# Attention and two MLPs on one core: the first batch of attention in program order on TensorE, with idle matmuls, the remaining weight decoding queued behind it, and half of the later normalizations on ScalarE

## The chip, the cores and the metric

One Trainium2 chip, one core. The time is device microseconds of one execution; the kernel before has a median of 905.58 us over 3 runs (903.2 to 906.58). The trace is that of one further, profiled execution.

## What is computed

Three stages, each on the output of the one before (2176 tokens, 512 features):

```
# attention: 4 batches x 8 heads, 512 local + 32 global positions, head size 64
s_l = [q_l k_g^T, q_l k_l^T within a window of 32]; out_l = softmax(s_l / 8) [v_g, v_l]
out_g = softmax(q_g [k_g, k_l]^T / 8) [v_g, v_l]
# first MLP: 512 -> 2048 -> 512; the weights arrive as float64
h = x @ w_in;  g = max(h, 0) + alpha * min(h, 0);  x = g @ w_out
# second MLP: 8 experts of 272 tokens each, tokens assigned greedily by x @ w_gate
out[mask_e] = max(x[mask_e] @ w1[e], 0) @ w2[e]
```

The softmax divides by the sum plus 1e-9: each row of exponentials is multiplied by a reciprocal. That multiplication is the "normalization" below.

## The kernel before

**Attention** works on 16 units, each two heads of one batch; four units make a batch (UPB = 4). A unit has two halves j of 256 queries. `attention()` (L473) is a generator that runs through steps n: scores of half n (`scores`, L356: four products, a fused scale, mask and row minimum on VectorE at L376, exponentials with row sums on ScalarE at L378), normalization of half n-1 (`norm`, L381: sum plus 1e-9, reciprocal, and four multiplications of 128x224 on VectorE at L389), transposes of half n-1 on TensorE with copies to SBUF on ScalarE (`ptrans`, L391), products with the values of half n-2 (`pv`, L402) and a copy to the batch's output tile XB. For every pair of units the global queries have a chain of their own, spread over four later steps by `todo` and `one()`: `gscores` (L412), `gnorm` (L429), `gtrans` (L435), `gpv` (L449). It goes to VectorE five times; `gpv` ends in a VectorE copy to XB (L461).

**The first MLP** runs on chunks of 272 tokens, two per batch (`gemm`, L175): a split of the input into a high half (ScalarE) and a low half (VectorE) at `splitx`, then eight slices f of a first product (`gemm1`, L158, 12 matmuls each, L167), each followed by two VectorE instructions (L172, L186) and a split (ScalarE and GpSimd), then a second product (L200), which needs all slices. It goes through half of the 2048 inner features at a time.

**Decoding**: the weights are float64 in memory. `decode` (L73) loads 128x512 of them as pairs of int32 (three raw buffers), takes the magnitude on ScalarE (L78), and puts a float32 together in four VectorE instructions (L79, L81, L82, L83; two magnitude buffers); `split` (L66) rounds on ScalarE and subtracts on GpSimd. `win_part` and `wout_part` are such decodings. The first half of the features needs 8 + 8 of them.

**Order**: batch 0 of the attention runs alone (`alone[0]`, with PSUM pools pS and pX of its own, and bank "y" of pY for the rest); in that loop (L531) four decodings are traced, one in six yields. Then a loop (L549) advances attention and MLP in turns and traces one of the twelve remaining decodings with each turn of the MLP. What is traced earlier has the higher priority, but the framework's planner orders each engine's queue by a timeline of its own: an instruction whose inputs are ready may be put ahead of ones traced before it, on TensorE as on VectorE. Each queue is then worked off in order. Loads and stores are issued by SyncE, also in order.

Of the kernel before, what the change touches and what calls it, by code (L numbers as in the profile page):

```python
# [11 lines left out]
BF = mybir.dt.bfloat16  # L12
# [3 lines left out]
OP = mybir.AluOpType  # L16
# [9 lines left out]
def tile_attention_moe_moe(ctx: ExitStack, tc: tile.TileContext, qkw, vw,  # L26
                           w_in, w_out, alpha, w_gate, w1, w2, out):
    nc = tc.nc
    V, A, P, T = nc.vector, nc.scalar, nc.gpsimd, nc.tensor
    B, H, S, D, SG = BHSDG  # L30
    DM, DF = w_in.shape
    E, _, FF = w1.shape
# [4 lines left out]
    KD = DM // 128  # L37
# [266 lines left out]
    with ExitStack() as at:  # L304
        mk = at.enter_context(tc.tile_pool(name="mk", bufs=1, side="right"))
# [4 lines left out]
        dc = at.enter_context(tc.tile_pool(name="dc", bufs=1, side="right"))  # L310
# [3 lines left out]
        alone = [True]  # L314
# [3 lines left out]
        def bank(shape, name):  # L318
            pool, tag = pY, "y"
            if not alone[0]:  # L320
                pool, tag = pA[0], "a"
            elif name == "s":
                pool, tag = ((pS, "s"), (pS, "s"), (pH, "h1"), (pH, "h1"))[turn[0] % 4]
                turn[0] += 1
            elif name == "t":
                pool, tag = pX, "x"
            return pool.tile(shape, F32, name=name, tag=tag)
# [3 lines left out]
        U = [dict() for _ in units]  # L331
# [14 lines left out]
        def load_v(u):  # L346
            d = U[u]
            vv = ld.tile([128, 2, NB, 2 * D], F32, name="vv", bufs=4)
            nc.sync.dma_start(out=vv.rearrange("p a i d -> p (a i d)"), in_=vw[u])
            d["va"], d["vb"] = vv[:, 0], vv[:96, 1]  # L350
# [30 lines left out]
        def norm(u, j):  # L381
            d = U[u]
            sm = d["sm"][:, :, 2 * j:2 * j + 2]
            V.tensor_scalar(sm, sm, 1e-9, None, op0=OP.add)
            V.reciprocal(sm, sm)
            for ii in range(2):
                i = 2 * j + ii
                for h in range(2):
                    V.tensor_scalar(d["pr"][:, h, i], d["pr"][:, h, i], d["sm"][:, h, i:i + 1], None, op0=OP.mult)  # L389

        def ptrans(u, j, half):  # L391
            d = U[u]
            n = 96 if half else 128
            t = bank([n, 2, 2, 128], "t")
            for ii in range(2):
                for h in range(2):
                    p = d["pr"][:, h, 2 * j + ii]
                    T.transpose(t[:, ii, h], p[:, 128:KW] if half else p[:, 0:128], ident)
            d["t", j, half] = tp.tile([n, 2, 2, 128], F32, name="pt", tag="bt" if half else "at")
            A.copy(d["t", j, half], t)  # L400

        def pv(u, j):  # L402
            d = U[u]
            o = bank([128, 2, 128], "o")
            for ii in range(2):
                i = 2 * j + ii
                for half, v in enumerate(("va", "vb")):
                    for h, c in heads(u):
                        T.matmul(o[c, ii], d[v][:, i, c], d["t", j, half][:, ii, h], start=half == 0, stop=half == 1)
            A.copy(d["x"][:, SG + 256 * j:SG + 256 * j + 256], o.rearrange("p i t -> p (i t)"))  # L410
# [58 lines left out]
            done[0] = 2 * p + 1  # L469

        done = [-1]

        def attention():  # L473
            todo = []

            def one():
                if todo:
                    x, f = todo.pop(0)
                    f()
                    yield x  # L480

            for n in range(2 * NU + 2):
                u, j = divmod(n, 2)
                if u < NU:
                    if j == 0 and u + 2 < NU:
                        load(u + 2)
                        load_v(u + 2)
                    scores(u, j)
                    yield 1.0
                if 1 <= n <= 2 * NU:  # L490
                    a_ = divmod(n - 1, 2)
                    norm(*a_)
                    ptrans(*a_, 0)
                    yield 0.45
                    ptrans(*a_, 1)
                    yield 0.45
                yield from one()
                if n >= 2:
                    pv(*divmod(n - 2, 2))
                    yield 1.0  # L500
                    v, j2 = divmod(n - 2, 2)
                    if v % 2 and j2:
                        gout(v // 2)
                        yield 0.1
                if u < NU and u % 2 == 0 and j:
                    p = u // 2
                    todo += [(0.8, lambda p=p: (gscores(p, 0), gscores(p, 1))), (0.0, lambda p=p: gnorm(p)),
                             (0.6, lambda p=p: (gtrans(p, 0), gtrans(p, 1))), (1.2, lambda p=p: gpv(p))]
# [2 lines left out]
        load(1)  # L511
        load_v(0)
        load_v(1)
        mask = mk.tile([128, 3, KW], F32, name="mask")
        P.memset(mask, 0.0)
        for i in range(3):
# [10 lines left out]
        UPB = H // 2  # L527
        parts = [(win_part, i) for i in range(2 * KD)]
        att = attention()
        n = 0  # L530
        while done[0] < UPB - 1:  # L531
            next(att)
            n += 1
            if n >= 6 and n % 6 == 0 and len(parts) > KD:
                f, i = parts.pop(0)
                f(dc, 0, i)
        nc.sync.dma_start(out=al, in_=alpha.rearrange("(f p) -> p f", p=128))
        nc.sync.dma_start(out=wg, in_=w_gate.rearrange("(k p) e -> p k e", p=128))
        parts += [(wout_part, i) for i in range(KH)]
        alone[0] = False  # L540
        first.close()
        pA.append(at.enter_context(tc.tile_pool(name="pA", bufs=4, space=PSUM)))
        loadx(0, 0)
# [5 lines left out]
        while going:  # L549
            want = c if g is None else c + 1  # L550
            if want < NCH and (want, 0) not in X and done[0] >= (want // CPB + 1) * UPB - 1 and (
                    g is None or len(X[c, 0]) == 4):
                loadx(want, 0)
            if g is None and (c, 0) in X:
                g = gemm(c, 0, None)
            if spent["a"] <= spent["g"] * ratio or g is None:
                x = next(att, None)
                if x is None:
                    going = False
                else:  # L560
                    spent["a"] += x
            else:
                x = next(g, None)
                if x is None:
                    g = None
                    c += 1
                else:
                    spent["g"] += x
                    if parts:
                        f, i = parts.pop(0)  # L570
                        f(dc, 0, i)

    wb = ctx.enter_context(tc.tile_pool(name="wb", bufs=1, side="right"))
    half_tiles(wb, "wb", 1)
# [1 line left out]
    with tc.tile_pool(name="dc2", bufs=1, side="right") as dc, tc.tile_pool(name="pW", bufs=2, space=PSUM) as pW:  # L576
        more = []
        parts = [(win_part, i) for i in range(2 * KD)] + [(wout_part, i) for i in range(KH)]
        n = 0
        while c < NCH:  # L580
# [4 lines left out]
            while next(g, None) is not None:  # L585
                n += 1
                if n % 3 == 0 and parts:
                    f, i = parts.pop(0)
# [12 lines left out]
    with ExitStack() as mo:  # L601
# [84 lines left out]
        for i, n in enumerate(TH + [1]):  # L686
            t = spot(n).bitcast(I32) if i else rc_.tile([128, n], I32, name="jt0")
# [488 lines left out]
        for k in range(E):  # L1176
            n = 0.0
# [86 lines left out]
```

## Time and profile before

| | |
|---|---|
| median of 3 runs | 905.58 us (903.2 to 906.58) |
| profiled execution | 907.86 us, of which the trace spans 906.1 us |
| busy: TensorE, VectorE, ScalarE, GpSimd | 852.9, 544.2, 404.5, 423.4 us |
| mean granted TensorE clock | 0.973 of full speed (2.4 GHz; the lower level is 0.50, 1.2 GHz) |
| DMA | 107.66 MB, mean 119 GB/s |

In the rows, PE is TensorE's matmul part, DVE is VectorE, ACT ScalarE, POOL GpSimd, SP SyncE. A row of the timeline gives the start and the duration in us, engine, line, operation, output <- input, shapes and count; in brackets stands how long the engine had been idle before and which engine's work ended the wait. A row that groups instructions gives the busy time in us and the mean of one in ns. L68 and L67 are the two lines of `split`.

### The profile page before, as it was taken

The page shows a single profiled execution, that of the slowest core. Times are in us where ns is not written, and L with a number is a line of the kernel's source. Part 1 is how long each engine was busy: PE and PEld are TensorE (multiplying, and loading weights), DVE is VectorE, ACT ScalarE, POOL GpSimd, SP SyncE. Part 2 cuts the span into 40 slices and gives each one's busy share as a digit, 9 for nine tenths or more (in the row PEclk, how much of TensorE's full clock was granted, in tenths as well). Part 3 has the DMA queues.
Part 4 walks back from the last instruction along what each step waited for, and adds up shares of the span by engine and source line. Part 5 has one row for each costly group of instructions (what it writes and reads, how often), then busy time and mean ns, then how long its engine had stood idle before and what let it go on. Part 6 is the DMA issues. An engine that isn't in the chain of part 4 may idle for free.

```text
span 906.1 us, 18734 instructions
## 1 busy us (share of the span) xinstructions
PE 852.9 (94%) x7168; PEld 779.2 (86%) x7168; DVE 544.2 (60%) x1783; ACT 404.5 (45%) x945; POOL 423.4 (47%) x367
## 2 busy tenths in 40 slices
PE   5979999999998899999999999999799999899996
PEld 3667888888887899999999899998498898899995
DVE  5999755565629984345555756677476666621120
ACT  5966654554534442233333334331244444444531
POOL 1234211110206543356666865652568678768721
PEclk8968999999999899999999999999999999999999
DMA  8575224223035522023220215332445555455510
GB/s 290 170 250 199 87 78 152 85 74 124 32 102 157 164 88 68 25 64 99 61 88 1 75 49 176 109 119 71 130 146 168 160 168 182 143 179 170 170 41 36
DMA packets 50273, 107.66 MB, mean 119 GB/s; under 512 B 6728, under 2 KB 23112, under 8 KB 50184
## 3 DMA queue, kind: packets, MB, share of 16 engines
q1 hardware_dynamic: 47288, 97.56, 34.4%
q0 software_dynamic: 2896, 8.92, 2.7%
q8 instruction: 56, 0.92, 0.4%
q14 instruction: 33, 0.27, 0.1%
HBM read 88.63 MB, written 17.83 MB: 117 GB/s over the span
## 4 chain that ended last, share of the span: by engine, by line
PE 30%; DMA 9%; POOL 8%; issue 5%; ACT 3%; DVE 2%; POOLq 0%; ACTq 0%
PE h L1106 11%; PE h L167 10%; DMA raw<-in_moe_w_dram 9%; POOL m L68 6%; PE lp L239 3%; ACT m L67 2%; PE h L980 2%; PE h L996 2%; POOL xg L931 1%; PE yt L228 1%; PE y L200 1%; PE pc L820 1%; DMA x2d<-yr 0%; POOL out_dram L1030 0%; PE pa L832 0%
## 5 line engine op out<-in xcount | busy, mean ns | idle before, releaser
L68 POOL TENSOR_TENSOR m<-raw,m 128x1024 fp32r<-128x1024 f32 x64 | 152.8, 2392 | 51.2 <-ACT m L67 50.7
L167 PE MATMUL h<-xh,win 128*128 128x272 f32 x768 | 168.6, 299 | 4.6 <-DVE g L186 2.7
L68 POOL TENSOR_TENSOR glo<-g,ghi 128x272 fp32r<-128x272 f32 x64 | 57.3, 898 | 193.1 <-ACT ghi L67 189.8
L167 PEld LDWEIGHTS h<-xh,win 128*128 128x128 f32 x768 | 128.8, 192 | 12.5 <-DVE g L186 4.4
L167 PE MATMUL h<-xl,win 128*128 128x272 f32 x384 | 112.7, 294 | 1.9 <-DVE xl L68 1.9
L200 PE MATMUL y<-ghi,wout 128*128 128x272 f32 x512 | 112.3, 299 | 2.1 <-ACT ghi L67 2.0
L172 DVE TENSOR_SCALAR nm<-h,al 128x272 f32<-128x272 f32 x128 | 63.4, 497 | 82.6 <-PE h L167 82.0
L1106 PE MATMUL h<-gr,wout 128*128 128x272 f32 x768 | 110.7, 295 | 0.4 <-POOL gr L68 0.4
L980 PE MATMUL h<-xsh,m 128*128 128x272 f32 x512 | 106.9, 298 | 2.0 <-ACT xsh L67 2.0
L67 ACT CAST m<-raw 128x1024 fp32r<-128x1024 f32 x64 | 66.9, 1048 | 85.8 <-DMA raw<-in_moe_w_dram 85.7
L996 PE MATMUL h<-hh,m 128*128 128x272 f32 x512 | 103.3, 293 | 0.0
L1106 PEld LDWEIGHTS h<-gr,wout 128*128 128x128 f32 x768 | 99.3, 188 | 1.3 <-POOL gr L68 0.7
L200 PEld LDWEIGHTS y<-ghi,wout 128*128 128x128 f32 x512 | 84.6, 190 | 6.1 <-ACT ghi L67 2.7
L980 PEld LDWEIGHTS h<-xsh,m 128*128 128x128 f32 x512 | 83.4, 191 | 3.0 <-ACT xsh L67 2.8
L996 PEld LDWEIGHTS h<-hh,m 128*128 128x128 f32 x512 | 81.4, 188 | 0.6 <-issue 0.4
L200 PE MATMUL y<-glo,wout 128*128 128x272 f32 x256 | 76.1, 300 | 2.8 <-POOL glo L68 2.8
L167 PEld LDWEIGHTS h<-xl,win 128*128 128x128 f32 x384 | 73.9, 192 | 2.9 <-DVE xl L68 2.6
L996 PE MATMUL h<-hl,m 128*128 128x272 f32 x256 | 75.6, 295 | 0.0
L980 PE MATMUL h<-xsl,m 128*128 128x272 f32 x256 | 75.5, 295 | 0.0
L378 ACT ACTIVATE pr<-sc,mx 128x224 f32<-128x224 f32 x128 | 60.4, 474 | 25.6 <-DVE mx L376 25.5
L68 POOL TENSOR_TENSOR l<-gb,h 128x272 fp32r<-128x272 f32 x62 | 54.5, 892 | 22.9 <-ACT h L67 22.2
L68 POOL TENSOR_TENSOR gr<-gb,gr 128x272 fp32r<-128x272 f32 x64 | 47.9, 774 | 32.9 <-ACT gr L67 32.8
(232 smaller groups left out, 1732.4 us busy)
## 6 DMA issues: line engine op xcount, KB each, us to landing
raw<-in_moe_w_dram SPq DMA_DIRECT2D x64, 512.0 KB, 3.6
qk<-in_qk_dram SPq DMA_DIRECT2D x15, 736.0 KB, 4.2
vv<-in_v_dram SPq DMA_DIRECT2D x16, 512.0 KB, 5.4
raw<-in_moe_w_in_dram SPq DMA_DIRECT2D x16, 512.0 KB, 5.6
raw<-in_moe_w_out_dram SPq DMA_DIRECT2D x16, 512.0 KB, 3.8
xs<-xb SPq DMA_DIRECT2D x16, 272.0 KB, 4.9
xpart<-xd SPq DMA_DIRECT2D x32, 136.0 KB, 1.8
xb<-xs SPq DMA_DIRECT2D x8, 544.0 KB, 4.2
```

Of the source, the lines that this page charges most:

```text
L67: a = A.copy(hi, src)
L68: return a, (lo_eng or V).tensor_tensor(lo, src, hi.bitcast(F32), op=OP.subtract)
L167: T.matmul(ps, wi[:, w, k, fs], x[:, k], start=i == 0, stop=i == 3 * KD - 1)
L172: V.tensor_scalar(nm, ps, 0.0, al[:, hf * KH + f:hf * KH + f + 1], op0=OP.min, op1=OP.mult)
L200: T.matmul(ps, wo[:, w, f, ds_], x[:, f], start=i == 0, stop=i == 3 * KH - 1)
L228: T.transpose(t[:, k * 128:(k + 1) * 128], tail["x"][:, k] if q == 2 else xo[:, k, a:b], ident)
L239: T.matmul(lp, w, x, start=first and i == 0, stop=last and i == 1)
L378: A.activation(out=d["pr"][:, h, i], in_=sc, func=AF.Exp, bias=d["mx"][:, h, i:i + 1], scale=-1.0, accum_out=d["sm"][:, h, i:i + 1])
L820: T.matmul(pc.rearrange("p a e -> p (a e)"), g[:, c:c + 2].rearrange("p a j -> p (a j)"), ohw[:, c:c + 2].rearrange("p a e -> p (a e)"), s ...
L980: T.matmul(ps, d["w1"][:, w, kk, fs], x[:, kk], start=i == 0, stop=i == 3 * KD - 1)
L996: T.matmul(ps, d["w2"][:, w, f, ms], x[:, f], start=i == 0, stop=i == 3 * K3 - 1)
L1106: T.matmul(ps[j], wo[:, w, f, ds_], x, start=f == 0 and a == 0, stop=f == KH - 1 and a == 2)
```

## The change

Batch 0's tracing loop is put under a manual schedule for TensorE, so that TensorE's instructions of this loop keep the order in which they are traced. While batch 0 is alone, `pad` traces idle matmuls (a zero matrix of 128x128 in bfloat16 times itself, repeated to 256 columns, into the unused half of the bank of the value products): 24 ahead of the first transposes, 12 ahead of the second, 3 ahead of each later one, and one ahead of each product with the values. The steps of the global queries move ahead of the normalization while batch 0 is alone. The decodings that are traced behind batch 0 for the first half of the features are issued behind the last normalization of batch 0 on VectorE. From batch 1 on and as long as such decodings are left to trace, ScalarE does the normalization of one of the two heads.

```diff
@@ norm @@
-                    V.tensor_scalar(d["pr"][:, h, i], d["pr"][:, h, i], d["sm"][:, h, i:i + 1], None, op0=OP.mult)
+                    p, r = d["pr"][:, h, i], d["sm"][:, h, i:i + 1]
+                    if h and share[0]:
+                        A.mul(p, p, r)
+                    else:
+                        at_norm[u, j] = V.tensor_scalar(p, p, r, None, op0=OP.mult)
@@ new functions; pv writes to obank(u, j)[:, 0] @@
+        def obank(u, j):
+            d = U[u]
+            if ("o", j) not in d:
+                d["o", j] = bank([128, 2, 2, 128], "o")
+            return d["o", j]
+
+        def pad(n, k):
+            if alone[0]:
+                t = obank(*divmod(n - 2, 2)) if n >= 2 else bank([128, 2, 2, 128], "o")
+                for _ in range(k):
+                    T.matmul(t[:, 1], zb, zb.unsqueeze(1).to_broadcast([128, 2, 128]), start=True, stop=True)
@@ attention @@
+                if alone[0]:
+                    yield from one()
                 if 1 <= n <= 2 * NU:
                     a_ = divmod(n - 1, 2)
                     norm(*a_)
+                    pad(n, PADS.get(n, 3))
                     ptrans(*a_, 0)
                     yield 0.45
                     ptrans(*a_, 1)
                     yield 0.45
-                yield from one()
+                if not alone[0]:
+                    yield from one()
                 if n >= 2:
+                    pad(n, 1)
                     pv(*divmod(n - 2, 2))
@@ ahead of the loops @@
+        PADS = {1: 24, 2: 12}
+        zb = mk.tile([128, 128], BF, name="zb")
+        V.memset(zb, 0.0)
@@ loop of batch 0 @@
-        while done[0] < UPB - 1:
-            next(att)
...
+        with tc.manual_schedule(engines={mybir.EngineType.PE}):
+            while done[0] < UPB - 1:
+                next(att)
...
         alone[0] = False
+        share[0] = True
@@ loop of attention and MLP in turns @@
                     if parts:
                         f, i = parts.pop(0)
-                        f(dc, 0, i)
+                        with tc.issue_after(at_norm[UPB - 1, 1].ins):
+                            f(dc, 0, i)
+                    else:
+                        share[0] = False
```

`issue_after` sets an order only: every VectorE instruction of the block is placed behind the named one in VectorE's queue. It adds no wait, and binds no other engine.

## Rows read from the trace of the kernel before

**Rows 1.** The page: the span, and the granted TensorE clock in tenths in 40 equal slices of it.

```profile
span 906.1 us, 18734 instructions
...
PEclk8968999999999899999999999999999999999999
```

**Rows 2.** Windows of 20 us: start and end, length, then for each engine the busy time in us and the number of instructions, the granted clock, the DMA engines' busy share, GB/s.

```profile
100.00:120.00 20.00, 20.00 (x208) 17.39 (x206) 11.70 (x52) 12.69 (x40) 1.99 (x2) 1.00 0.53 177
...
240.00:260.00 20.00, 20.00 (x178) 17.51 (x175) 9.38 (x38) 10.99 (x32) 1.23 (x1) 1.00 0.11 37
```

**Rows 3.** The same view, cut where the granted clock changes: length, then PE, PEld, DVE, ACT and POOL busy, clock, DMA share, GB/s.

```profile
0.00:17.90 17.90, 9.98 (x56) 6.66 (x56) 8.16 (x44) 7.54 (x23) 3.93 (x18) 1.00 0.89 327
17.90:24.80 6.90, 5.06 (x30) 3.67 (x32) 6.83 (x25) 6.04 (x21) 1.56 (x1) 0.52 0.72 177
24.80:48.70 23.90, 20.34 (x195) 13.85 (x191) 23.90 (x97) 21.11 (x68) 5.46 (x4) 1.00 0.62 197
48.70:55.00 6.30, 5.77 (x32) 4.60 (x32) 6.30 (x21) 5.53 (x15) 1.28 (x1) 0.50 0.81 315
55.00:65.20 10.20, 8.92 (x86) 7.50 (x85) 9.93 (x15) 5.58 (x10) 3.86 (x3) 0.50 0.52 152
65.20:69.70 4.50, 1.80 (x13) 1.30 (x11) 4.43 (x7) 2.60 (x5) 1.33 (x1) 0.88 0.93 285
69.70:75.80 6.10, 6.10 (x24) 5.30 (x26) 6.00 (x22) 4.74 (x13) 2.04 (x2) 0.50 0.80 273
75.80:95.00 19.20, 18.84 (x145) 15.82 (x142) 19.20 (x51) 10.91 (x28) 9.07 (x9) 1.00 0.35 122
```

**Rows 4.** TensorE's timeline: the first products, a wait in batch 0, and the first products of the MLP that others follow.

```profile
4.40 3.30 PE L370 MATMUL s<-qk 64*128 64x224 f32 x16 [4.40 <-DMA qk<-in_qk_dram]
...
46.96 1.10 PE L409 MATMUL o<-pt,vv 128*64 128x128 f32 x16 [2.69 <-DVE gmx L423]
...
69.67 0.60 PE L167 MATMUL h<-xl,win 128*128 128x272 f32 x1 [1.65 <-DVE xl L68]
```

**Rows 5.** VectorE's timeline: mask of the second pair's global scores, copy of their result, low half of the MLP's input.

```profile
46.21 0.69 DVE L423 CUSTOM_DVE_ANT_0 gsc<-gs,gmask 128x512 f32<-128x512 f32 x1
...
65.72 0.22 DVE L461 COPY xb<-go 128x64 f32<-128x64 f32 x1
...
68.34 1.28 DVE L68 TENSOR_TENSOR xl<-xb,xh 128x1088 fp32r<-128x1088 f32 x1
```

**Rows 6.** VectorE from 0 to 95 us by instruction and shape (busy us, mean ns): the four instructions of a decoding and the first of the two MLP operations; below, the window of 0 to 55 us for the last instruction of a decoding (L83) alone: length, VectorE busy and count, clock, DMA.

```profile
L82 DVE SCALAR_TENSOR_TENSOR mag<-raw,mag 128x512 int32<-128x512 int32 x16 | 15.1, 944 | 0.2
L83 DVE SCALAR_TENSOR_TENSOR mag<-raw,mag 128x512 int32<-128x512 int32 x16 | 11.0, 685 | 0.1
L81 DVE TENSOR_SCALAR mag<-mag 128x512 int32<-128x512 int32 x16 | 10.2, 635 | 0.2
L79 DVE TENSOR_SCALAR mag<-mag 128x512 f32<-128x512 f32 x16 | 6.9, 430 | 1.7 <-ACT mag L78 1.7
...
L172 DVE TENSOR_SCALAR nm<-h,al 128x272 f32<-128x272 f32 x5 | 2.4, 485 | 0.0
...
0.00:55.00 55.00, 4.41 (x7) 0.88 0.74 250
```

**Rows 7.** TensorE's timeline at clock 1.00: scores of one step, four of the eight transposes of one step, value products of one step, global products with the values and global scores of one pair.

```profile
26.13 1.03 PE L370 MATMUL s<-qk 64*128 64x224 f32 x8
27.10 0.64 PE L398 MATMUL t<-ident,pr 128*96 128x128 f32 x4
...
32.30 1.10 PE L409 MATMUL o<-pt,vv 128*64 128x128 f32 x16
...
36.05 1.36 PE L458 MATMUL go<-gt,vv 128*64 128x32 f32 x40
...
41.42 1.24 PE L421 MATMUL gs<-qk 128*64 128x512 f32 x8
```

**Rows 8.** The window of 75.8 to 95 us, one line of the kernel at a time (length, busy and count on its engine, for TensorE of matmuls and weight loads, clock, DMA): L370 scores (8 a step), L398 transposes (8 a step), L409 value products (16 a step), L83 last instruction of a decoding.

```profile
75.80:95.00 19.20, 4.35 (x16) 2.59 (x16) 1.00 0.35 122
75.80:95.00 19.20, 2.23 (x16) 1.73 (x16) 1.00 0.35 122
75.80:95.00 19.20, 2.15 (x32) 1.74 (x32) 1.00 0.35 122
75.80:95.00 19.20, 2.71 (x4) 1.00 0.35 122
```

**Rows 9.** Prices: 24 products of 272 columns of the MLP as the chain that ended last has them (start us, us); then, from 0 to 95 us by instruction and shape (busy us, mean ns), the exponential, the copy of the value products, and the normalization.

```profile
420.50 3.02 PE h L167 x24
...
L378 ACT ACTIVATE pr<-sc,mx 128x224 f32<-128x224 f32 x49 | 23.2, 475 | 9.2 <-DVE mx L376 9.1
...
L410 ACT COPY xb<-o 128x256 f32<-128x256 f32 x10 | 3.6, 361 | 0.0
...
L389 DVE TENSOR_SCALAR pr<-pr,sm 128x224 f32<-128x224 f32 x48 | 15.8, 387 | 0.1
```

**Rows 10.** Timelines of VectorE and GpSimd: the third instruction of a decoding, and the subtractions of two decodings that follow one another.

```profile
60.05 1.73 DVE L82 SCALAR_TENSOR_TENSOR mag<-raw,mag 128x512 int32<-128x512 int32 x1
...
59.95 1.28 POOL L68 TENSOR_TENSOR win<-mag,win 128x512 fp32r<-128x512 f32 x1 [2.53 <-ACT win L67]
63.24 1.29 POOL L68 TENSOR_TENSOR wout<-mag,wout 128x512 fp32r<-128x512 f32 x1 [2.01 <-ACT wout L67]
```

More of the change, by code (lines that the diff above doesn't have):

```diff
@@ L400, in ptrans @@
             A.copy(d["t", j, half], t)
+        def obank(u, j):
[8 more added lines that the diff above has]
+                    T.matmul(t[:, 1], zb, zb.unsqueeze(1).to_broadcast([128, 2, 128]), start=True, stop=True)
         def pv(u, j):
             d = U[u]
-            o = bank([128, 2, 128], "o")
+            o = obank(u, j)[:, 0]
             for ii in range(2):
@@ L471, in tile_attention_moe_moe @@
         done = [-1]
+        share, at_norm = [False], {}
         def attention():
@@ L530, in tile_attention_moe_moe @@
         n = 0
-        while done[0] < UPB - 1:
-            next(att)
-            n += 1
-            if n >= 6 and n % 6 == 0 and len(parts) > KD:
-                f, i = parts.pop(0)
-                f(dc, 0, i)
+        with tc.manual_schedule(engines={mybir.EngineType.PE}):
+            while done[0] < UPB - 1:
+                next(att)
+                n += 1
+                if n >= 6 and n % 6 == 0 and len(parts) > KD:
+                    f, i = parts.pop(0)
+                    f(dc, 0, i)
         nc.sync.dma_start(out=al, in_=alpha.rearrange("(f p) -> p f", p=128))
@@ L570, in tile_attention_moe_moe @@
                         f, i = parts.pop(0)
-                        f(dc, 0, i)
+                        with tc.issue_after(at_norm[UPB - 1, 1].ins):
+                            f(dc, 0, i)
+                    else:
+                        share[0] = False
     wb = ctx.enter_context(tc.tile_pool(name="wb", bufs=1, side="right"))
```

## The prediction

> **What bounds the kernel now.** I read the page first: the span is 906.1 us, and the granted TensorE clock has its dents in the first tenth and a few later slices [rows 1]. The windows of 20 us then show where TensorE is simply full: from about 95 us until the attention is over it is busy 20.00 of 20 us at clock 1.00 [rows 2]. Time won before 95 us therefore shifts everything behind it, and time won inside the full stretch would need less TensorE work, which the change doesn't bring. So the question is how much TensorE time is lost before 95 us, and by what.
>
> I cut that part where the granted clock changes [rows 3] and count as lost the length of a stretch minus busy time times clock: 7.9 us (0 to 17.9), 4.3, 3.6, 3.4, 5.7, 2.9, 3.1 and 0.4 us. The sum is 31.2 us, 19.2 of them up to 55 us and 12.0 behind. The first product waits for its load until 4.40 us; a wait of 2.69 us on VectorE sits at 46.96; the first product of the MLP that is followed by others starts at 69.67 [rows 4].
>
> In the same stretches VectorE is busy 84.74 of 95 us, practically without a gap after 17.9 us [rows 3]. Its queue is in order, so a short chain that crosses it several times becomes long: the global queries of the second pair of units pass VectorE first at 46.21 (mask) and last at 65.72 us (copy of the result), and the low half of the MLP's input is made at 68.34 [rows 5]. What stands between is decoding of weights: of sixteen decodings seven have come to their last instruction by 55 us [rows 6]. One decoding is four VectorE instructions of 430 + 635 + 944 + 685 ns, 2.69 us [rows 6]; sixteen are 43 us, half of what VectorE does by 95 us.
>
> **The change, part by part.**
>
> *Decodings behind the last normalization of batch 0.* Four decodings are traced inside batch 0 and stay; twelve now go behind. No semaphore wait is added, only an order on VectorE. The decodings' other steps (load by SyncE, absolute value and rounding on ScalarE, subtraction on GpSimd) keep their places, but there are three raw and two magnitude buffers, so loads beyond these wait for VectorE, and on SyncE's queue the query, key and value loads can stand behind such a load. For batch 0 itself VectorE has 45.2 us of work by 55 us [rows 3]; without about 6.6 decodings (17.7) that is 27.5. One normalization too many (four of 387 ns, 1.5 [rows 9]) goes off, two copies like the one of 0.22 [rows 5] are still to come (0.5), and four decodings (10.8) are added: 37.3 us. Idle time of VectorE was 9.8 us up to 55; I take 3 us more, since TensorE in program order feeds it less freely. Batch 0 then leaves VectorE at 37.3 + 12.8 = 50.1 us.
>
> *TensorE in program order.* Full-clock prices are 1.03 us for the scores of one step, 2 x 0.64 for its transposes, 1.10 for its value products, and 1.24 + 1.36 for a global pair [rows 7], whose five transposes cost about 0.8. Ten, nine and eight steps and two pairs make 10.3 + 11.5 + 8.8 + 6.8 = 37.4 us. In program order the two heads' scores always stand next to each other; that is worth something where they were split (two later steps took 4.35 us for their scores instead of 2.06 [rows 7, 8]), and I count it in the 37.4 only.
>
> *Idle matmuls.* These are 24 + 12 + 7 x 3 + 8 = 65 of 256 columns, in bfloat16. The trace has none. Nearest is the product of 272 columns, 24 in 3.02 us at full clock, 0.126 us each [rows 9]; at half clock twice that. All 65 cost 8 to 16 us if nothing covered them and nothing if all fall into waits. The waits of this part are larger (16 us below), but the first 24 come when TensorE is not yet quick and can hold back the first transposes by up to 3 us. A gain is not excluded: they can keep the clock where it now falls to 0.50 at 17.9 and 48.7 us [rows 3]. I take 1.5 us of cost, nearer to the covered end because 55 - 41.16 us of TensorE stood idle up to 55 even now; batch 0 then ends at 51.6 us on VectorE.
>
> Between the last copy at 65.72 and the product at 69.67 lie 3.95 us now; with a queue that holds decodings I take 3.3, so the MLP starts at 55 us, where TensorE has lost 55 - 37.4 = 17.6 us. That is 1.6 less than now at 55 us, but with the whole of batch 0 done, and the MLP 14.7 us earlier.
>
> *ScalarE takes half of the normalizations behind batch 0.* VectorE is spared two of 387 ns per step [rows 9], about 0.5 us in the queue. ScalarE pays between 361 (its copy of 256 columns) and 475 ns (its exponential, same shape, with a pointer operand) each [rows 9]; I take 475, because of the operand. ScalarE is busy 10.91 of 19.2 us in the last stretch [rows 3], so this is hidden unless the transposes wait for it; without that cover it is 0.9 us per step.
>
> *After batch 0.* VectorE must do twelve decodings (32.3), eight pairs of MLP operations (about 2 x 0.485 [rows 6], 7.3) and the low half (1.3): 40.9 us, so decoding ends at 92.5 us plus what attention steps take there. The 27.5 us above hold ten steps and nearly two global pairs, 2.75 us a step all told; with half of the normalizations gone, 2.25. TensorE can do meanwhile the first MLP product of a chunk (96 at 0.126, 12 us) and some 5 us of the second one, which needs every decoding before it can finish, and per attention step 2.18 + 1.12 + 1.08 us as measured between 75.8 and 95 us [rows 8] plus 0.85 of a pair: 5.25 us. With a steps in that time it loses 92.5 + 2.25a - 55 - 17 - 5.25a = 20.5 - 3a us. Everything hangs on a. In the order of the code a is about 2.5; in the last stretch now, two steps pass beside four decodings [rows 8], which gives 6 beside twelve. I take 4.5, nearer to the row: 7.0 us lost.
>
> **Sum.** 17.6 + 7.0 = 24.6 us against 31.2, a gain of 6.6. The profiled execution took 907.86 us (span 906.1), 2.3 above the median of 905.58; 901.3 against its own time, 899.0 against the median. I forecast **899 us**.
>
> **The rivals.** *VectorE's work is only moved (no change).* Decoding pulled forward was not wasted: the same 43 us must pass VectorE before the second product of the MLP can end. With a = 3 the loss after batch 0 is 11.5 us and the gain 2.1: 903.5. For it: VectorE was full before and after. Against it: from 55 to 69.7 us now VectorE does almost nothing but decode, while TensorE idles or runs at half clock. To this rival also belongs that idle matmuls don't hold the clock, or that the first 24 lie on the path.
>
> *The decodings become a wall (slower).* Released together they may be issued one behind the other with the attention behind them; a = 2.5, TensorE loses 13.0 us and, without idle matmuls after batch 0, half its clock too. In a row they are also dearer: while GpSimd subtracts for 1.28 us, the third instruction of the next decoding takes 1.73 us [rows 10], where the fourth, of the same kind and size, takes 0.685 [rows 6], and they follow each other every 3.29 us [rows 10] instead of 2.69. Twelve times 0.60 are 7.2 us; the time is 17.6 + 13.0 + 7.2 - 31.2 = 6.6 us worse, 912.2. It decides as soon as fewer than three steps pass among twelve decodings. The Trainium skill, "SBUF — State Buffer" (Who interferes with whom), states that a VectorE instruction with two SBUF inputs and a GpSimd instruction that reads SBUF exclude each other for the whole instruction; the 1.73 us beside the 1.28 agree. By that rule every decoding next to another pays, and the sum would be this rival's; the mean of 2.69 over all sixteen says that among attention steps most of it is avoided.
>
> *TensorE stays full (faster still).* With a = 6.8 nothing is lost after 55 us, and with idle matmuls for nothing the loss is 16.1: 15.1 us gained, 890.5. For it: from 75.8 to 95 us both engines are full together [rows 3].
>
> **How the numbers follow.** Forecast 0.43, TensorE full 0.15, only moved 0.22, wall 0.20. The bounds of the idle matmuls (0 to 3 us more) and a between 3.5 and 5.5 put the forecast's own case at 894.5 to 903.5. The range reaches to 890 and 911, with the far halves of the outer cases left out. About 4.5 us, 0.5%, is what a measurement can tell: faster 0.55 (the full case and most of the forecast's), same 0.25, slower 0.20.
>
> **What would show it.** Right: the first run of MLP products near 55 us; clock 1.00 through batch 0; the last copy of the global pair a few us behind its transposes; no decoding but four before the last normalization of batch 0; the last of sixteen decodings at about 103 us; TensorE busy and at full clock from 60 us on. Wrong: TensorE idle, or at 0.50, between 55 and 90 us with decodings in a row on VectorE (wall); the MLP starting after 62 us (program order or the 24 matmuls on the path); a change that arises behind 260 us, which this sum doesn't contain.

## The result, and the profile after

The changed kernel is slower: a median of 910.26 us in 8 runs against 905.5 in 8 of the kernel before, a ratio of 1.0066 (95% interval 1.0042 to 1.009). The forecast was 899.0, faster. (Medians are over all runs of a kernel; the ratios compare undisturbed runs only and are not the quotients of these medians, so the change is 4.8 us by the one and 6.0 by the other.) The profiled execution took 908.36 us, of which the trace spans 906.3.

The page's span and granted clock, against [rows 1]: the first tenth has no 6 any more.

```profile
span 906.3 us, 18854 instructions
...
PEclk8899999999999899999999999999999999999998
```

The windows of [rows 3], cut at the same times, and one more up to 120 us (length; PE, PEld, DVE, ACT, POOL busy; clock; DMA share, GB/s):

```profile
0.00:17.90 17.90, 9.91 (x64) 7.38 (x65) 5.42 (x29) 6.39 (x20) 3.93 (x18) 0.96 0.91 330
17.90:24.80 6.90, 3.20 (x16) 2.47 (x16) 6.80 (x24) 4.76 (x15) 1.82 (x1) 0.50 0.63 158
24.80:48.70 23.90, 19.37 (x195) 14.55 (x194) 19.41 (x71) 17.97 (x52) 4.09 (x3) 0.89 0.54 161
48.70:55.00 6.30, 6.30 (x71) 5.13 (x69) 3.80 (x21) 5.00 (x16) 0.00 (x0) 1.00 0.79 282
55.00:65.20 10.20, 7.22 (x93) 5.52 (x90) 10.13 (x39) 8.10 (x26) 2.64 (x2) 0.95 0.31 101
65.20:69.70 4.50, 4.50 (x36) 3.89 (x35) 4.43 (x10) 3.69 (x8) 0.00 (x0) 0.74 0.68 243
69.70:75.80 6.10, 6.10 (x51) 5.67 (x50) 5.99 (x17) 3.78 (x10) 4.10 (x4) 1.00 0.75 262
75.80:95.00 19.20, 17.66 (x147) 15.12 (x145) 19.17 (x57) 13.82 (x40) 8.37 (x8) 1.00 0.48 168
95.00:120.00 25.00, 22.43 (x204) 18.00 (x202) 24.05 (x66) 15.12 (x39) 9.58 (x7) 1.00 0.43 138
```

Length minus busy time times clock, as in the prediction, gives 8.4, 5.3, 6.7, 0.0, 3.3, 1.2, 0.0, 1.5 and 2.6 us: 29.0 lost, 2.2 less than the 31.2 of before, which lost nothing between 95 and 120 us. But the busy time holds 65 idle matmuls, which compute nothing. Twelve of them behind one another are 1.49 us at full clock (in a row of an experiment below), 0.12 each, so 65 are about 8 us of full-clock work. With them the useful work lost is about 37 us, some 6 more than before. Whether they bring the better clock, the run without them shows below. VectorE shows the other side: by 55 us it has worked 5.42 + 6.80 + 19.41 + 3.80 = 35.4 us against 45.2 [rows 3], and it is still full between 95 and 120 us (24.05 of 25 us), where the sixteenth decoding ends at last.

TensorE's timeline of the changed kernel, batch 0 and the first products of the MLP (columns as in [rows 4]):

```profile
4.49 3.36 PE L370 MATMUL s<-qk 64*128 64x224 f32 x16 [4.49 <-DMA qk<-in_qk_dram]
7.78 3.61 PE L416 MATMUL o<-zb 128*128 128x256 bf16 x24
11.23 1.04 PE L402 MATMUL t<-ident,pr 128*128 128x128 f32 x8
...
13.15 1.25 PE L437 MATMUL gs<-qk 128*64 128x512 f32 x8
21.60 2.72 PE L416 MATMUL o<-zb 128*128 128x256 bf16 x12 [7.20 <-DVE gmx L439]
24.11 1.91 PE L402 MATMUL t<-ident,pr 128*128 128x128 f32 x8
...
67.95 0.52 PE L167 MATMUL h<-xh,win 128*128 128x272 f32 x2
```

Read the fifth line. The twelve idle matmuls write into the bank of the value products, where the global scores (13.15) still lie, so they wait 7.20 us until VectorE has read these (L439), and the transposes behind them, already fed, wait too. Twelve idle matmuls then run at 0.227 us each, at half clock: the wait that they were to bridge is their own. In the kernel before only the value products wait for that bank [rows 4], behind the transposes. The MLP starts at 67.95 us; the prediction had 55.

VectorE reads the global scores so late because its queue has the first decoding in front of them, and stands until that decoding's load and magnitude are done:

```profile
18.00 0.43 DVE L79 TENSOR_SCALAR mag<-mag 128x512 f32<-128x512 f32 x1 [4.02 <-ACT mag L78]
...
20.86 0.68 DVE L439 CUSTOM_DVE_ANT_0 gsc<-gs,gmask 128x512 f32<-128x512 f32 x1
```

TensorE's waits by line from 0 to 70 us (total us, times, longest), before and after:

```profile
PE s L370 <- DMA qk<-in_qk_dram: 4.4, 1, 4.4
PE o L409 <- DVE gmx L423: 3.5, 2, 2.7
PE s L370 <- DVE mx L376: 3.0, 2, 2.7
PE t L398 <- ACT pt L400: 2.9, 2, 2.6
```

```profile
PE o L416 <- DVE gmx L439: 8.1, 2, 7.2
PE s L370 <- DMA qk<-in_qk_dram: 4.5, 1, 4.5
PE t L402 <- DVE pr L393: 4.0, 3, 1.6
PE o L416 <- ACT gt L463: 2.1, 2, 1.6
```

Before, no transposes stand among the waits for a normalization (pr); after, idle matmuls wait 10.2 us for banks and transposes 4.0 us for normalizations.

VectorE's timeline of the changed kernel, from the last normalization of batch 0 on, with GpSimd's subtractions in the second fence:

```profile
55.21 1.07 DVE L393 TENSOR_SCALAR pr<-pr,sm 128x224 f32<-128x224 f32 x4
...
60.18 0.68 DVE L83 SCALAR_TENSOR_TENSOR mag<-raw,mag 128x512 int32<-128x512 int32 x1
...
60.85 0.69 DVE L83 SCALAR_TENSOR_TENSOR mag<-raw,mag 128x512 int32<-128x512 int32 x1
...
62.76 2.10 DVE L393 TENSOR_SCALAR pr<-pr,sm 128x224 f32<-128x224 f32 x4
64.78 0.21 DVE L477 COPY xb<-go 128x64 f32<-128x64 f32 x1
...
66.61 1.28 DVE L68 TENSOR_TENSOR xl<-xb,xh 128x1088 fp32r<-128x1088 f32 x1
...
115.41 0.68 DVE L83 SCALAR_TENSOR_TENSOR mag<-raw,mag 128x512 int32<-128x512 int32 x1
```

```profile
61.60 2.64 POOL L68 TENSOR_TENSOR win<-mag,win 128x512 fp32r<-128x512 f32 x2 [22.87 <-ACT win L67]
```

The order on VectorE holds: four decodings stand inside batch 0, and the next two behind its last normalization (55.21). But the copy of the global result (64.78) is later than that normalization, and these two decodings and the normalization of the next batch (62.76) pass in front of it. The last decoding ends at 116.1 us instead of 94.5. All sixteen, in the changed kernel from 0 to 120 us (busy us, mean ns), against [rows 6]:

```profile
L82 DVE SCALAR_TENSOR_TENSOR mag<-raw,mag 128x512 int32<-128x512 int32 x16 | 13.5, 851 | 0.1
L83 DVE SCALAR_TENSOR_TENSOR mag<-raw,mag 128x512 int32<-128x512 int32 x16 | 12.3, 767 | 0.0
L81 DVE TENSOR_SCALAR mag<-mag 128x512 int32<-128x512 int32 x16 | 8.4, 525 | 0.1
L79 DVE TENSOR_SCALAR mag<-mag 128x512 f32<-128x512 f32 x16 | 7.6, 480 | 4.8 <-ACT mag L78 4.8
```

480 + 525 + 851 + 767 = 2.62 us a decoding, against 2.69: queued up they are not dearer.

### The profile page after: what moved, and what is told of

Same layout as the page of the kernel before. It is cut to its first block, busy times and chain, and to the rows that moved or that the text cites. A ratio compares the mean times of both kernels' runs of the same rounds, so it can differ in the third digit from the quotient of the medians.

```text
span 906.3 us, 18854 instructions
## 1 busy us (share of the span) xinstructions
PE 850.0 (94%) x7233; PEld 778.9 (86%) x7233; DVE 542.3 (60%) x1780; ACT 407.2 (45%) x949; POOL 426.5 (47%) x367
## 4 chain that ended last, share of the span: by engine, by line
PE 36%; POOL 6%; DMA 5%; issue 5%; ACT 2%; DVE 2%; POOLq 0%; ACTq 0%
PE h L1136 11%; PE h L167 10%; DMA raw<-in_moe_w_dram 5%; PE h L1010 5%; POOL m L68 4%; PE h L1026 4%; PE lp L239 3%; ACT m L67 1%; POOL xg L961 1%; PE yt L228 1%; PE y L200 1%; POOL out_dram L1060 1%; PE pc L850 1%; PE xt L996 0%; DMA x2d<-yr 0%
## 5 line engine op out<-in xcount | busy, mean ns | idle before, releaser
L167 PE MATMUL h<-xh,win 128*128 128x272 f32 x768 | 165.8, 296 | 2.6 <-DVE g L186 1.9
L200 PE MATMUL y<-ghi,wout 128*128 128x272 f32 x512 | 113.5, 300 | 1.4 <-ACT ghi L67 1.3
L200 PEld LDWEIGHTS y<-ghi,wout 128*128 128x128 f32 x512 | 85.1, 191 | 5.5 <-issue 2.7
L200 PE MATMUL y<-glo,wout 128*128 128x272 f32 x256 | 75.3, 299 | 3.4 <-POOL glo L68 3.4
```

The costliest lines, as they stand in the source:

```text
L167: T.matmul(ps, wi[:, w, k, fs], x[:, k], start=i == 0, stop=i == 3 * KD - 1)
L200: T.matmul(ps, wo[:, w, f, ds_], x[:, f], start=i == 0, stop=i == 3 * KH - 1)
```

## Experiments

Ratios are to the kernel before, timed beside each group of experiments (its medians there are 906.8, 907.1, 906.2 and 906.6 us).

**Theory.** The loss is batch 0: in program order TensorE stands still where VectorE is late, VectorE then gets its work later and idles, and the idle matmuls add waits and time; queueing and ScalarE's half are no loss. **Rivals:** the queued decodings form a wall behind batch 0; the late load of the first decoding (VectorE waits 4.02 us for it before L79 at 18.00) holds up the start; the loss arises behind the first half of the MLP, since the last of its second product's weight loads (L200) starts at 390.90 us before and at 392.82 after, only 1.9 us later.

**Without idle matmuls, and with them in another bank.**

```diff
 # no_idle
-            if alone[0]:
+            if False:
                 t = obank(...)
 # idle_in_t: those ahead of the transposes write into the transposes' own bank
-                    pad(n, PADS.get(n, 3))
-                    ptrans(*a_, 0)
+                    ptrans(*a_, 0, PADS.get(n, 3))
```

> The changed kernel without its idle matmuls, all else kept. Theory (the idle matmuls hold TensorE: they take the bank of the value products ahead of the transposes and wait there for VectorE and ScalarE to read the global scores out of it, 10.2 us in the trace of the changed kernel, 7.2 of them in one wait at 14.4 us): the transposes of the second step start by 16 us instead of 24.1, the first MLP product comes before 64 us instead of 67.95, and the time is 3 to 6 us below the changed kernel, about that of the kernel before (903 to 907). Rival (batch 0 is late because VectorE, without the decodings, waits in step with TensorE's program order): the first MLP product stays within 2 us of 68 and the time within 2 us of 910. Second rival (the idle matmuls do hold the clock): TensorE falls to 0.50 in batch 0 and the time is above 912.

> The changed kernel with the same number of idle matmuls, but those ahead of the transposes write into the transposes' own bank instead of that of the value products. Theory (it is the bank, not the matmuls): the wait of 7.2 us ahead of the second group disappears, the first MLP product comes before 64 us, the clock is at 1.00 longer than without idle matmuls, and the time is 4 to 7 us below the changed kernel (903 to 906). Rival (the first decoding's late load holds ScalarE and VectorE until 17.3 us whatever TensorE does): TensorE waits for ScalarE's copies instead until about 18 us, and the gain is at most 2 us.

Without them 909.28 us (1.0019, 0.9996 to 1.0042), in the other bank 907.99 (1.0016, 0.9997 to 1.0036), against 1.0063 to 1.0066 of the changed kernel. Both edits take about 4 us off. The timeline of the second shows what went, and what came instead (the first groups, the two later waits, the MLP's start):

```profile
7.87 2.99 PE L401 MATMUL t<-zb 128*128 128x256 bf16 x24
...
13.80 1.49 PE L401 MATMUL t<-zb 128*128 128x256 bf16 x12
15.12 0.60 PE L405 MATMUL t<-ident,pr 128*128 128x128 f32 x4
...
33.60 2.06 PE L405 MATMUL t<-ident,pr 128*128 128x128 f32 x8 [3.27 <-DVE pr L393]
...
61.29 2.07 PE L405 MATMUL t<-ident,pr 128*128 128x128 f32 x8 [3.48 <-DVE pr L393]
...
65.41 0.82 PE L167 MATMUL h<-xh,win 128*128 128x272 f32 x2
```

The twelve come at 13.80 at full clock instead of 21.60, with no wait ahead of them. In the transposes' bank the same matmuls cost nothing that can be told, though the MLP starts at 65.41, not before 64 as expected. It is the bank, more than the matmuls themselves, that costs. Without any of them the MLP starts at 60.39, 7.6 us earlier, and the time follows only by half.

The kernel without idle matmuls (no_idle) also shows what they do to the clock. Its first transposes, and two of the windows above:

```profile
9.97 1.98 PE L402 MATMUL t<-ident,pr 128*128 128x128 f32 x8 [2.16 <-DVE pr L393]
...
17.90:24.80 6.90, 4.79 (x45) 3.50 (x44) 6.90 (x27) 6.05 (x18) 1.29 (x1) 1.00 0.82 237
48.70:55.00 6.30, 5.61 (x58) 4.31 (x58) 6.30 (x23) 3.94 (x12) 0.62 (x1) 0.73 0.09 11
```

The first transposes take 1.98 us here and 1.04 behind the 24 idle matmuls (11.23 above), so these do quicken TensorE. After that the gain is gone: from 17.9 to 24.8 us the clock is 1.00 without idle matmuls and 0.50 with them, from 48.7 to 55 us 0.73 without and 1.00 with them, and the granted clock of the whole execution has a median of 0.978 in both kernels. The better clock against the kernel before is not theirs. Nor does TensorE wait here for a bank that VectorE must read: VectorE reads the global scores at 15.69, ahead of the first decoding.

**Program order alone, and everything but program order.**

```diff
 # before_order: the kernel before, and
-        while done[0] < UPB - 1:
+        with tc.manual_schedule(engines={mybir.EngineType.PE}):
+            while done[0] < UPB - 1:
 # planner_pe: the changed kernel, and
-        with tc.manual_schedule(engines={mybir.EngineType.PE}):
+        if True:
```

> The kernel before with one part alone: TensorE in program order while batch 0 is alone. Theory (TensorE in program order can't step over an instruction that waits, and with decodings free to go ahead on VectorE each step waits for them): the first MLP product comes after 75 us and the time is 4 to 10 us above the kernel before. Rival (the run without queueing was slow through its idle matmuls): within 3 us of the kernel before.

> The changed kernel, but TensorE's order in batch 0 left to the planner; idle matmuls, queueing and ScalarE's half stay. Theory (program order with the idle matmuls' bank is what makes batch 0 last until 68 us): the first MLP product comes before 64 us, and the time is 3 to 6 us below the changed kernel (904 to 907). Rival (the planner puts the idle matmuls, which need nothing but a bank, wherever a bank is free, and their bank still makes the others wait): within 2 us of the changed kernel or above it.

The order alone makes the kernel before 1.0183 (1.0163 to 1.0202), 924.1 us: 17 us, where 4 to 10 were expected. Its largest wait from 0 to 70 us (total, times, longest):

```profile
PE t L398 <- DVE pr L389: 17.5, 7, 4.9
```

Seven groups of transposes wait 17.5 us for normalizations, which stand behind decodings on VectorE; in the kernel before no such wait stands up to 70 us. Given back to the planner, the changed kernel takes 904.53 us (0.9978, 0.9961 to 0.9995). There the first 24 idle matmuls run at 1.00 us, ahead of all data, and the MLP starts at 59.86.

**The queued decodings and ScalarE's half.**

```diff
 # free_decode: the changed kernel, and
-                        with tc.issue_after(at_norm[UPB - 1, 1].ins):
-                            f(dc, 0, i)
+                        f(dc, 0, i)
 # no_share: the changed kernel, and
-        share[0] = True
 # before_queue: the kernel before, and the lines that free_decode takes out
 # queue_share: before_queue, and the lines on share
 # queue_share_globals: queue_share, and one() ahead of norm() in batch 0
```

> The changed kernel without the order that puts the twelve decodings behind the last normalization of batch 0. Theory (VectorE is the bound up to the last decoding, and holding decodings back leaves it idle in batch 0: 35.4 us busy by 55 us against 45.2 in the kernel before): the last decoding ends before 100 us instead of 116, TensorE is full from 95 us on, and the time is 2 to 5 us below the changed kernel (905 to 908). Rival (the queueing helps, the order on TensorE harms): batch 0 ends later than 68 us and the time is above 912.

> The changed kernel with all normalizations on VectorE. Theory (VectorE is full from 55 to 116 us, about six steps fall into that time, half a us each): the last decoding ends 2 to 4 us later and the time is 1 to 3 us above the changed kernel (911 to 913). Rival (ScalarE's half is dearer, 0.95 us per step in an engine whose queue the transposes wait for): the time is 1 to 3 us below it (907 to 909).

> The kernel before with one part alone: the twelve decodings queued behind the last normalization of batch 0. Theory (VectorE's decoding work is only moved: what TensorE wins early it waits for later): the first MLP product comes 6 to 10 us earlier than in the kernel before (69.67), the last decoding ends after 103 us instead of 94, and the time is within 2 us of the kernel before. Rival (holding them back is a gain of its own, as the run without it suggests, which was 8 us slower than the changed kernel): 4 us or more below the kernel before. Second rival (VectorE idles in batch 0 and never catches up): 3 us or more above it.

> The kernel before with the queueing of the decodings and ScalarE's half, TensorE left to the planner, no idle matmuls. Theory (queueing alone gave 2.8 us, and VectorE was still full from 68 to 95 us and the last decoding late; ScalarE's half relieves just that stretch): 4 to 7 us below the kernel before (900 to 903). Rival (ScalarE's half is worth nothing, as in the changed kernel, where it made no difference in time): as queueing alone, 2 to 3.5 us below.

> As the run with queueing and ScalarE's half, with the global queries' steps moved ahead of the normalization as well: the changed kernel without program order and idle matmuls. Theory (the move makes the long chain of the second pair end sooner): the first MLP product comes 1 to 2 us earlier than without it, and the time is 0 to 2 us lower. Rival (the planner orders by readiness whatever the order of tracing): within 1 us of it. Against the run that has idle matmuls too but no program order, it shows what these cost: theory 0 to 2 us.

| kernel | median us | ratio, 95% interval | last decoding's last instruction |
|---|---|---|---|
| free_decode | 918.31 | 1.0126, 1.0102 to 1.015 | 88.20 |
| no_share | 911.95 | 1.0059, 1.0037 to 1.0082 | 122.00 |
| before_queue | 904.14 | 0.9969, 0.9945 to 0.9994 | 111.43 |
| queue_share | **902.53** | 0.995, 0.9929 to 0.997 | 107.17 |
| queue_share_globals | 903.43 | 0.9966, 0.9941 to 0.999 | 106.82 |

The wall falls: queueing alone is a gain of 2.8 us with the last decoding 18 us later than before, and taking it out of the changed kernel costs 5 to 6 us more, with the last decoding earliest of all; the gain of 2 to 5 us expected there was a loss. ScalarE's half brings that last decoding forward by 4 to 7 us; the time falls by 1.7 us beside the queue (overlapping intervals), and by nothing that can be told in the changed kernel. It is a small part: in the whole trace of the changed kernel ScalarE does four normalizations, those of one head in two steps, from 67.1 to 79.7 us (busy us, mean ns):

```profile
L391 ACT ACTIVATE pr<-pr,sm 128x224 f32<-128x224 f32 x4 | 1.7, 477 | 0.4 <-DVE sm L385 0.4
```

The flag `share[0]` goes back while the program is traced, as soon as the twelve decodings are handed out, and these run long after that. Four instructions less are 1 to 2 us for VectorE (0.27 to 0.53 each); why the last decoding moves by more is not shown.

The early global steps do nothing measurable. queue_share beats both kernels. With queue, share and early globals in all of them, program order makes 0.9966 into 1.0019 (no_idle), 4.8 us, with intervals that just keep apart.

**The late first load.**

```diff
-                if n >= 6 and n % 6 == 0 and len(parts) > KD:
+                if n >= 12 and n % 6 == 0 and len(parts) > KD:
                     f, i = parts.pop(0)
-                    f(dc, 0, i)
+                    with tc.issue_after(at_copy[0, 1].ins):
+                        f(dc, 0, i)
```

In late_decode this edits the changed kernel, in queue_share_late queue_share (at_copy is ScalarE's copy of the transposes).

> The changed kernel with the first decodings of batch 0 queued on each engine's way behind ScalarE's copy of the second step's transposes (ScalarE's part alone is bound by it). Theory (ScalarE and, behind it, VectorE stand before the first decoding's load until 17.3 us, so TensorE's wait of 5.8 to 7.2 us ahead of the second group of idle matmuls is the load's): that wait falls below 2 us, the first MLP product comes 4 to 6 us earlier (61 to 64 us), and the time is 2 to 5 us below the changed kernel. Rival (the steps' own order sets the pace, four decodings must pass in batch 0 in any case): the wait falls but the first MLP product moves by less than 2 us, and the time by less than 2 us.

> The run with queueing and ScalarE's half, with the first decodings queued on ScalarE behind the copy of the second step's transposes. Theory (the first load's late landing holds ScalarE and VectorE for about 2 us each in the planner's order too): TensorE's waits between 13 and 20 us (2.3 + 2.1 us) shrink to under 2 in sum and the time is 1 to 3 us lower than without it. Rival (VectorE must do the same work by the last decoding): within 1 us.

909.81 us (1.0045, 1.0028 to 1.0062) and 903.64 (0.9969, 0.9953 to 0.9986): some 2 us less in the one, with overlapping intervals, and 1 to 2 more in the other. That rival falls as the main cause. In late_decode the twelve start at 15.84 after a wait of 0.99 us, as expected, but the MLP starts at 68.62, later than in the changed kernel. So the 7.20 us of that wait are not 7.20 us of time: what is won there is mostly waited for elsewhere in batch 0.

**The changed kernel again.**

> The changed kernel itself, for a second trace and beside the others. Its eight executions lay between 908.29 and 916.65 us, wider than those of the kernel before, and the trace is of a quick one. Theory (its in-order waits for the first decoding's load make it depend on when loads land): the start of the first MLP product and the end of the attention differ between its two traces by over 1 us. Rival (the spread comes from the experts' part): the two traces agree within 0.5 us up to 390 us and differ behind.

912.37 us (1.0063, 1.0047 to 1.008). The wait ahead of the twelve is 5.76 us instead of 7.20, the MLP starts at 66.93, and the last L200 load at 392.42, 0.4 us from the first trace; yet this execution took 911.73, 3.4 us more. So single traces vary by that much behind 390 us, and a trace can't place the loss of 5 us.

**The first 400 us by themselves.** Four kernels were ended behind the first half of the first MLP; the second half and the experts are left out.

```diff
+    flat = out.rearrange("a d -> (a d)").rearrange("(k p t) -> k p t", k=KD, p=128)
+    for k in range(KD):
+        nc.sync.dma_start(out=flat[k], in_=xpart[k])
+    g1.close()
+    gm.close()
+    return
     NDEF = 8
```

> The kernel before, ended behind the first half of the first MLP (its second half and the experts are left out; the partial sums are copied to the output). The scale for the three others, some 405 to 430 us: the last second product's weight load of the full kernel starts at 390.9 us, and some stores and a copy of 4.5 MB follow.

> The changed kernel ended at the same place. If the extra 5 to 6 us of the changed kernel's median arise ahead of this place (batch 0 in program order with idle matmuls): 4 to 7 us above before_cut. If most of them arise behind it, in the second half of the MLP and the experts, as the traces suggest (392.8 against 390.9 us at the landmark): 1 to 3 us above before_cut.

> The changed kernel without idle matmuls, ended at the same place. If the full kernels' medians arise ahead of this place: 1 to 3 us above before_cut (full: 1.7 above) and about 4 below changed_cut. If they arise behind it: within 1.5 us of before_cut, as the traces' landmarks are (390.1 against 390.9 us).

> The kernel before with the queued decodings and ScalarE's half alone, ended at the same place. If its gain of 4.5 us arises ahead of this place: 3 to 6 us below before_cut. If behind it: within 1.5 us of before_cut, as the landmarks are (391.3 against 390.9 us).

| kernel, ended there | median us | ratio to the full kernel before, 95% interval |
|---|---|---|
| before_cut | 403.23 | 0.4446, 0.4436 to 0.4456 |
| changed_cut | 406.75 | 0.4484, 0.4465 to 0.4504 |
| no_idle_cut | 406.58 | 0.4466, 0.4448 to 0.4484 |
| queue_share_cut | 399.67 | 0.4408, 0.4388 to 0.4427 |

The changed kernel is 3.5 us behind and queue_share 3.6 ahead in this part, with intervals apart from that of before_cut: most of both effects arises here. The other 2 us of the changed kernel may lie behind it or within the uncertainty; that stays open. no_idle_cut lies between, 1.8 us behind by its ratio, and is not told from either.

The end of batch 0 on TensorE in queue_share_cut, where the planner orders it:

```profile
44.63 1.10 PE L413 MATMUL o<-pt,vv 128*64 128x128 f32 x16 [2.59 <-DVE gmx L427]
45.66 0.64 PE L402 MATMUL t<-ident,pr 128*96 128x128 f32 x4
46.23 1.10 PE L413 MATMUL o<-pt,vv 128*64 128x128 f32 x16
47.26 1.09 PE L402 MATMUL t<-ident,pr 128*128 128x128 f32 x8
51.80 1.12 PE L450 MATMUL gt<-ident,gsc 128*128 128x128 f32 x4 [3.44 <-DVE gsc L437]
...
60.93 0.50 PE L167 MATMUL h<-xh,win 128*128 128x272 f32 x2
```

Value products and transposes of several steps come one behind the other, ahead of the global pair's transposes (gt, 51.80), which wait 3.44 us. The MLP starts at 60.93 us, 6 us ahead of changed_cut's (66.86), without an idle matmul and with no wait of transposes for a normalization among its waits up to 65 us.

## Why the prediction was wrong

Three steps failed: the time at which batch 0 leaves VectorE, the price of program order on TensorE, which the forecast held in a clause, and the price of the idle matmuls. Queueing, ScalarE's half and the early global steps together are a small gain (0.9966); program order adds 4.8 us and the idle matmuls 4, which is the loss.

*What bounds the kernel* held in outline: most of the effect lies in the first part. No single landmark does it. The two kernels whose MLP starts latest are the slowest (before_order at 82.41 us, free_decode at 80.89), but the changed kernel starts it 1.7 us earlier than the kernel before and is slower, and queueing makes the last decoding later and the kernel faster.

*Batch 0 leaves VectorE at 51.6 us*: this step failed; it was 64.9 us (the copy at 64.78). By then VectorE had worked 45.3 us (35.4 up to 55 us by the windows above, and 9.9 behind, without a gap) where I had 37.3, and idled 19.6 where I had 12.8 and 1.5 for idle matmuls: 8.0 + 5.3 are the 13.3 us. The work first: "behind the last normalization of batch 0" is not behind batch 0. Two queued decodings (4.3 us from 56.20 to 61.5) and the normalization of the next batch (2.10, and 0.3 for its sum and reciprocal) came in front of the global copy, since the global chain outlasts that normalization; that is most of the 8.0. The idle time next. "I take 3 us more, since TensorE in program order feeds it less freely" was a number without a row. The order alone costs 17 us with decodings in the way, and 4.8 with them held back: no smaller than the idle matmuls, as far as the intervals tell, and the prediction gave it a clause.

*Idle matmuls, 1.5 us*: they cost 4 us. The bounds of 0 to 16 us contained it, and the choice near the covered end was wrong because it asked only whether TensorE is idle at that time, not what the idle matmul itself must wait for. They were counted as fillers of waits and became the wait: 10.2 us of it, of which about 4 arrive in the time. The gain that was not excluded came for the first transposes (1.04 us instead of 1.98) and not at 17.9 (0.50, before 0.52), where they themselves stand still; at 48.7 us the clock is 1.00 (before 0.50), but without idle matmuls it is 0.73 there. That matmuls can't pass one another is also what the Trainium skill states, on the page "PSUM — Partial Sum Buffer" (Engine vs sequencer instructions): they start and complete in program order. The rows agree: no transposes start between 13.15 and 21.60.

*From the copy to the MLP, 3.3 us*: 64.78 to 67.95, 3.2. Right, though no row gave the 3.3.

*After batch 0* TensorE was to lose 7.0 us with a = 4.5. It lost 4 to 5 (1.5 and 2.6 us from 75.8 us on, and part of the 1.2 before). Between 65.8 and 116.1 us TensorE has 40 score products, five steps, and VectorE ends ten decodings, so a is about 6 beside twelve, what [rows 8] said. The middle between code and row was needless here; but for 6 the prediction's formula gives 2.5 us, so it was not exact either.

*ScalarE's half*: 477 ns an instruction (475 taken), but only two steps had it, where the half microsecond was counted for each of 4.5 steps; the time gained 1.7 us at most.

*The sum*: 17.6 us lost before the MLP and 7.0 behind made 24.6. It was some 32 us (24 by the windows, 8 of idle matmuls) and 4 to 5: 37, against 31.2. The 6 us that this gives are close to the 5 to 6 that were measured (3.5 in the cut kernels), but that is partly luck: the same sum over the trace of no_idle gives 27.1 us, 4 less than before, where its ratio is 1.7 us more. So such a sum over one trace can be off by 6 us. One reason stands in the rows: the recorded clock of the first stretch is 1.00, yet sixteen score products take 3.30 us at 4.40 [rows 4] and eight take 1.03 at 26.13 [rows 7]; the 7.9 us that the prediction read there are too few.

*The rival that came true in its sign* was not the wall: neither fewer than three steps nor dearer decodings are in the trace. The rule cited for it, of the page "SBUF — State Buffer" (Who interferes with whom) of the Trainium skill, still agrees in places: at 70.31 us one L82 takes 1.72 us beside a subtraction of 1.31. It does not set the sum, at 2.62 us a decoding. The prediction's remark "the MLP starting after 62 us (program order or the 24 matmuls on the path)" named the true failure, but inside the rival of no change; it had no price of its own.

## What to carry to other kernels

A filler in an in-order queue has a wait of its own: look up which buffer it writes, who still reads that, and what stands behind it. Fixing an engine's order is a change to every wait on that engine; price it by the work that the planner now slips into each of them, as the chain of waits shows it. And when work is ordered behind "the last" instruction of a stage, check that this is the last one: here another chain beside it ended 8.7 us later. Count in the trace, too, how many instructions a part of the change touches: ScalarE's half was four.

## What had not been expected of the hardware

Four normalizations on VectorE took 1.07 us at 55.21 and 2.10 at 62.76, where GpSimd subtracts (61.60 to 64.24). They are not all slower: three of the four took 0.32 to 0.33 us, as each does at 55.21, and one, begun at 63.0, took 1.36, to just behind the end of the subtractions:

```profile
L393 DVE TENSOR_SCALAR pr<-pr,sm x4: 324/329/1357, 62.8 to 64.5; 128x224 f32<-128x224 f32 x4
```

(Shortest, median and longest in ns, first and last start.) The same happens at 23.48 beside a subtraction at 22.89: one of 1.36 us among four. The mean of 387 ns in [rows 9] mixes the two; its 48 have a median of 328 and a longest of 1379 ns.

Without program order 24 idle matmuls at 1.00 us, ahead of all data, take 4.37 us, and the scores behind them 1.78 us for sixteen products instead of 3.36: idle matmuls do quicken TensorE, where nothing else could run and their bank is free. The recorded clock of this stretch is 1.00 in both kernels; only the durations tell them apart. That kernel has no better ratio (0.9978) than the one without them (0.9966).
